# Leaving one half of an inverse transform mirrored, in a kernel of windowed attention beside a long convolution

## The chip, the cores and the metric

The kernel runs on one core of a Trainium2 chip. Its engines have instruction queues of their own and wait for one another by semaphores: TensorE (PE: matrix products, with its weight loads listed as PEld), VectorE (DVE), ScalarE (ACT), GpSimd (POOL) and SyncE (SP). SP, ACT and POOL can start DMA transfers; only those that POOL starts can add to what is in the memory they write. The metric is device time in microseconds (us), as the median of runs.

## The reference

Two independent heads are computed and laid side by side in the output, A in columns 0 to 575, B in columns 576 to 1151. A is attention over a dilated window of 8 keys; B is a convolution along the sequence, by Fourier transforms, times q.

```python
def _A_ref(x, wqkv, wo):
    B, S, D = x.shape
    H = 32; Dh = D // H
    W, dil = 8, 2
    ...
    q, k, v = qkv[0], qkv[1], qkv[2]
    ...
    logits = jnp.einsum("bhsd,bhswd->bhsw", q, kg) * scale
    logits = jnp.where(mask[None, None, :, :], logits, -1e9)
    attn = _softmax(logits, axis=-1)
    o = jnp.einsum("bhsw,bhswd->bhsd", attn, vg)
    return (lambda x, *d: x.transpose(*d))(o, 0, 2, 1, 3).reshape(B, S, D) @ wo

def _B_ref(q, k, v, shift_k, ssm_k, ssm_D):
    ...
    for t in range(ks):
        k_shift = k_shift + k_pad[:, t:t + S, :] * shift_k[:, ks - 1 - t][None, None, :]
    kv = k_shift * v
    L = 2 * S
    ...
    y_f = kv_f * kf_f[None, :, :, :]
    y = (lambda x, s, axes=(-2,-1): jnp.fft.irfft2(x, s=s, axes=axes).astype(jnp.bfloat16))(y_f, (1, L), axes=(1, 2))[:, 0, :S, :]
    y = y + kv * ssm_D[None, None, :]
    return q * y
```

Here kg and vg are the keys and values of the window, gathered by position, and kv_f and kf_f the Fourier transforms of kv and ssm_k, padded to twice the length.

## The kernel before

Everything stays in SBUF. Large tiles are reused by hand: xw, Ks, qk, av, v and TB hold other things in each stage, and a stage that wants a region waits until its last reader is done.

**Head A** runs in the first three quarters: projections (ps_proj), products of q and shifted k on DVE (`logits`) summed over a head by PE (ps_log), softmax, weights of attention spread over partitions by DMA (`spread`), products with v on DVE (`weigh`), summed by PE (ps_acc), and the output product (ps_wo, `outputs`). The two factors of a `weigh` product are v and a spread tile X, and X lies by turns in TB, Ks and qk.

**Head B** cuts the sequence into NBL = 4 blocks of 512 rows. Input blocks (kv, in xw) and filter blocks (in Ks) are folded by their mirror symmetry (`mirror`, `fold_filter`), transformed by PE with a table TX or TK (`x_spectrum`: ps_fx, `filter_spectrum`: ps_fk), and stored as two halves, real and imaginary, a and b. A complex product is done with three real ones, and needs a third array c = a + b of each spectrum, its "third": K0 to K3 are those of Ks, X0 to X3 those of xw. A third is made either on DVE (`add_third`, or in `produce`, line 1244, where it is first needed) or by transfers (`third`, lines 1050 to 1055): SP copies a over c, then POOL adds b to c by an accumulating DMA. The table THIRDS says which, PRE at which step DVE makes those of part 0.

`spectral` then works through output blocks j = 0 to 3, three column groups t of each, and for each the products i = 0 to j: DVE multiplies xw's spectrum i with Ks's spectrum j − i (`products`, line 1099, 2304 elements a partition), into one of a few "homes", regions that have become free, in turn; PE sums them over i into ps_z with identity matrices (`sum_of`, line 1126, 16 matrix products each), ACT copies the sum to Y (line 1139). DVE is up to three products ahead of PE. "Block 2's third product" means i = 2 of j = 2, t = 0.

`inverse` takes Y back to time. With E the transform of the one half of Y and O of the other, the first 256 rows of a block are E + O and the last 256 are E − O in mirrored order. PE first makes E in ps_inv, ACT copies it to A; PE adds O on top, and ACT copies E + O to y[0:2]. Then `back` makes the last rows on PE: with matrices of a flipped identity, flip2 · A − flip · y = flip · (2E − (E + O)) = flip · (E − O), in ps_back, which ACT copies to y[2:4] (line 1206). DVE multiplies by q (the "gate", line 1212) and SP stores the block. For block 3 the columns are done as 384 and 192, the last 192 by `last`, which makes E and O in two PSUM tiles and both halves by ps_back; `gate_last` multiplies straight from PSUM.

The order of work is written by hand: `units` is a queue of PE work (with labels: inv, wo, fx, fk), and `until()` takes from it, at each place where it is called, as many as the next number of the table PLACES. `tasks` holds the gates, done once their time is due by a rough clock; block 2's gate waits in `late` until the last product is made. The steps 1 to 26 of the main loop go through `weigh`, start further spreads and outputs, and from step 21 on run pieces of `spectral` by the table ZMIX. FKS and FXS mix the spectra's units, REGROUP and AT place other pieces. `load_q` loads the blocks of q by POOL, into TB, which is free once the last X in it has been read.

Of the kernel before, what the change touches and what calls it, by code (L numbers as in the profile page):

```python
# [12 lines left out]
ALU = mybir.AluOpType  # L13
# [6 lines left out]
    2, 1, 1, 0, 1, 4,  # L20
# [3 lines left out]
    25, 22,  # L24
)

THIRDS = ((0, 1),), ((0, 2), (1, 2)), ((0, 3), (1, 3))

REGROUP = (
    15, 14,  # L30
# [3 lines left out]
    2, 14, 13, 4, 3, 0, 2, 4, 8, 2, 10, 2, 6, 1, 4, 4, 3, 6, 1, 3, 0, 5, 5, 5, 3, 3, 4, 2, 1, 0, 3, 11, 2, 2, 3,  # L34
    1, 1, 4, 0, 10, 0, 3, 0, 2, 11, 1, 1, 0,
# [3 lines left out]
    5, 1, 0, 0, 0, 0, 0, 0, 0, 0, 0, 0, 0, 0, 0, 3, 0, 0, 0, 0, 0, 0, 0, 0, 0, 0, 0, 0, 0, 0,  # L39
)  # L40
FXS = (
    0, 0, 15, 0, 8, 0, 0, 4, 0,
# [7 lines left out]
    1, 5, 19,  # L50
# [9 lines left out]
def kernel(  # L60
# [186 lines left out]
    def turn_x(h):  # L247
# [15 lines left out]
    flip = main.tile([128, 128], BF16, name="flip")  # L263
    nc.gpsimd.affine_select(flip[:], ones128[:], pattern=[[1, 128]], compare_op=ALU.is_equal, fill=0.0,
                            base=-127, channel_multiplier=1)
# [6 lines left out]
    flipn = main.tile([128, 128], BF16, name="flipn")  # L272
    nc.gpsimd.tensor_scalar(flipn[:], flip[:], -1.0, None, op0=ALU.mult)
# [7 lines left out]
    flip2 = main.tile([128, 128], BF16, name="flip2")  # L281
    nc.gpsimd.tensor_scalar(flip2[:], flip[:], 2.0, None, op0=ALU.mult)
# [371 lines left out]
    def negate(*ms):  # L654
        for m in ms:
            signed.add(m)
            dve(288, lambda: nc.vector.tensor_scalar(minus_of(m), spare(m) if m < 2 else row(m, 0), -0.5 * ROOT, None,
                                                     ALU.mult))
# [384 lines left out]
    def outputs(hh, c):  # L1043
        for sb in (2 * hh, 2 * hh + 1):
            for h in range(2):
                units.append((1.15, partial(output, c, sb, h), "wo"))
# [3 lines left out]
    def third(x, n):  # L1050

        moved.add((bool(x), n))
# [19 lines left out]
    def upper(t, j, a, width, c0, n):  # L1072

        return bass.AP(tensor=t.tensor, offset=t.offset + (BL * j + 320 - 64 * a) * width + c0,
                       ap=[[width, 64], [(64, 192)[a] * width, 2], [1, n]])

    def store_b(j, c0, n, src, h):
        other = nc.scalar if j == NBL - 1 else nc.sync
        if h == 0:
# [266 lines left out]
```

## Time and profile before

| | us |
|---|---|
| three runs | 212.08, 213.55, 212.07 |
| median | 212.08 |
| profiled execution, whole | 212.5 |
| its span | 210.8 |
| ACT busy | 150.5 (71%) |
| POOL busy | 74.0 (35%) |
| DMA, mean rate | 188 GB/s |

The granted clock of PE was 0.998 in the profiled execution. In the profile's rows a line L1099 is line 1099 of the listing above; `out<-in` names tiles; a bracket at the end of a row is the time for which the engine stood idle before it and what ended that, as the profile infers it from semaphores. A row that merges several instructions gives the first one's start and their busy time. The "chain" is the work that ended last, followed back from the end, step by step to what released it. A row of SPq, ACTq or POOL with DMA in it is the issue of a transfer; "to landing" is the time from there until its data are in place.

### The profile page before, as it was taken

What the parts mean: (1) busy time and instruction counts of PE and PEld (TensorE: products, weight loads), DVE (VectorE), ACT (ScalarE), POOL (GpSimd) and SP (SyncE); (2) the same over time, 40 slices, a digit from 0 to 9 for tenths busy, and PEclk for the clock granted to TensorE, in tenths of its full rate; (3) what the DMA queues carried; (4) which work ended last, traced back from release to release, by engine and by line L of the source; (5) the groups of instructions that cost most, each with busy time, mean ns of one, the idle gap of its engine ahead of it and who ended that gap; (6) DMA issues with size and microseconds to landing.
All of it is one profiled execution on the core that took longest, in us unless ns stands there. A gap on an engine that the chain in (4) does not pass through costs nothing.

```text
span 210.8 us, 5106 instructions
## 1 busy us (share of the span) xinstructions
PE 200.1 (95%) x2114; PEld 110.7 (53%) x2122; DVE 193.1 (92%) x146; ACT 150.5 (71%) x218; POOL 74.0 (35%) x111
## 2 busy tenths in 40 slices
PE   7999999999999999899999999999989999999891
PEld 2443443344554656564354666656555666666460
DVE  7989999999999999858889999999999849999981
ACT  3799988657684989986369788855666796775540
POOL 8999993001195516320175000002029004033000
PEclk9999999999999999999999999999999999999999
DMA  6999998999639336999999997587559995985133
GB/s 201 303 328 231 266 342 280 170 192 182 151 75 122 48 40 87 180 181 171 235 225 238 194 234 159 105 208 185 153 223 255 239 322 110 214 243 182 28 113 111
DMA packets 35396, 39.66 MB, mean 188 GB/s; under 512 B 17619, under 2 KB 29007, under 8 KB 35374
## 3 DMA queue, kind: packets, MB, share of 16 engines
q1 hardware_dynamic: 26812, 24.88, 47.2%
q0 software_dynamic: 6096, 11.96, 30.4%
q10 hardware_dynamic: 2466, 2.51, 3.5%
q8 instruction: 16, 0.26, 0.5%
q14 instruction: 6, 0.05, 0.1%
HBM read 13.11 MB, written 4.72 MB: 85 GB/s over the span
## 4 chain that ended last, share of the span: by engine, by line
PE 80%; ACT 10%; DVE 5%; issue 2%; DVEq 0%; ACTq 0%
PE ps_proj L378 16%; PE ps_z L1126 9%; PE ps_wo L1029 8%; PE ps_acc L973 7%; PE ps_inv L1158 7%; PE ps_fx L776 6%; PE ps_log L847 4%; PE ps_proj L500 3%; PE ps_fk L627 3%; PE ps_proj L382 3%; PE ps_proj L389 3%; ACT Ks L695 3%; PE ps_rev L673 2%; PE ps_fk L628 1%; ACT qk L977 1%
## 5 line engine op out<-in xcount | busy, mean ns | idle before, releaser
L378 PE MATMUL ps_proj<-xw 128*128 128x512 bf16 x153 | 37.4, 380 | 0.6 <-issue 0.3
L832 DVE TENSOR_TENSOR av<-qk 128x4096 bf16<-128x4096 bf16 (+1 forms) x16 | 31.7, 2013 | 2.8 <-PE ps_log L847 2.8
L378 PEld LDWEIGHTS <-xw 128*128 128x128 bf16 x160 | 14.0, 97 | 20.5 <-issue 6.2
L1099 DVE TENSOR_TENSOR qk<-xw,Ks 128x2304 bf16<-128x2304 bf16 x14 | 18.5, 1355 | 2.5 <-PE ps_inv L1158 2.4
L1139 ACT ACTIVATE av<-ps_z 128x768 bf16<-128x768 f32 x20 | 15.3, 808 | 6.2 <-PE ps_z L1126 6.2
L414 ACT ACTIVATE qk<-ps_proj 128x1024 bf16<-128x1024 f32 x14 | 14.3, 1023 | 7.6 <-PE ps_proj L389 3.3
L695 ACT ACTIVATE Ks<-ps_fk 128x576 bf16<-128x576 f32 x32 | 18.6, 717 | 1.3 <-PE ps_fk L628 1.3
L577 DVE TENSOR_TENSOR tB<-kj,skb 128x4608 bf16<-128x4608 bf16 (+1 forms) x8 | 19.3, 2417 | 0.1
L778 ACT ACTIVATE xw<-ps_fx 128x576 bf16<-128x576 f32 x32 | 18.4, 666 | 0.0
L776 PE MATMUL ps_fx<-xw,TB 128*128 128x288 bf16 x128 | 18.0, 286 | 0.2
L1055 POOL DMA_DIRECT2D Ks<-Ks x3 | 3.7, 1218 | 41.1 <-PE ps_wo L1029 28.7
L1029 PE MATMUL ps_wo<-qk 128*128 128x288 bf16 x128 | 17.8, 287 | 0.0
L627 PE MATMUL ps_fk<-Ks,TB 128*128 128x384 bf16 x62 | 16.9, 326 | 0.8 <-ACT Ks L695 0.7
L414 ACT ACTIVATE v<-ps_proj 128x1024 bf16<-128x1024 f32 x9 | 9.3, 1029 | 9.3 <-PE ps_proj L378 4.3
L973 PE MATMUL ps_acc<-av,ident 64*64 64x512 bf16 x160 | 15.3, 377 | 0.0
L628 PE MATMUL ps_fk<-Ks,TB 128*128 128x192 bf16 x62 | 15.2, 245 | 0.0
L776 PEld LDWEIGHTS <-TB 128*128 128x128 bf16 x128 | 12.0, 97 | 6.0 <-issue 2.9
L1029 PEld LDWEIGHTS <-qk 128*128 128x128 bf16 x128 | 11.6, 98 | 5.6 <-issue 3.0
L1158 PE MATMUL ps_inv<-av,TI 128*128 128x288 bf16 (+1 forms) x96 | 13.6, 293 | 0.6 <-ACT av L1139 0.6
L1161 ACT ACTIVATE v<-ps_inv 128x576 bf16<-128x576 f32 (+1 forms) x14 | 9.5, 677 | 6.3 <-PE ps_inv L1158 6.3
L977 ACT ACTIVATE qk<-ps_acc 128x1024 bf16<-128x1024 f32 x8 | 8.2, 1024 | 8.0 <-PE ps_acc L973 8.0
L956 DVE TENSOR_TENSOR av<-Ks,v 128x4096 bf16<-128x4096 bf16 x6 | 13.6, 2286 | 0.2 <-PE ps_acc L973 0.2
(199 smaller groups left out, 471.3 us busy)
## 6 DMA issues: line engine op xcount, KB each, us to landing
Ks<-Ks POOLq DMA_DIRECT2D x9, 576.0 KB, 7.1
TB<-av SPq DMA_DIRECT2D x12, 256.0 KB, 5.5
kj<-in_B_k_dram SPq DMA_DIRECT2D x6, 504.0 KB, 6.1
vt<-in_B_v_dram SPq DMA_DIRECT2D x8, 288.0 KB, 5.2
Ks<-av SPq DMA_DIRECT2D x8, 256.0 KB, 5.5
Ks<-Ks SPq DMA_DIRECT2D x3, 576.0 KB, 6.1
Ks<-in_A_x_dram SPq DMA_DIRECT2D x2, 576.0 KB, 5.2
xw<-in_A_wqkv_dram SPq DMA_DIRECT2D x2, 576.0 KB, 5.9
```

Source lines behind the costliest of these rows:

```text
L378: nc.tensor.matmul(ps[:, jp, :], wq(kb, comp, 128 * ct, 128), xT(kb, 1024 * jj + 512 * jp, 512), **se)
L414: nc.scalar.activation(view(t, o + pad + 1024 * jj, [[512, 2], [1, 512]]), ps[:], ACT.Copy)
L577: dve(2304 * n, lambda: nc.vector.tensor_tensor(to, view(kj, row * D, [[D, n], [D, 4], [1, D]]), view(skb, row * D, [[D, n], [0, 4], [1, D ...
L627: nc.tensor.matmul(o[:, 0:2], w, rhs[:, 0:2], start=start, stop=stop)
L695: nc.scalar.activation(view(Ks, k_at(m, cs ^ (m & 1)) + 96 * gi, [[768, 3], [384, 2], [1, 96]]), acc3(ps), ACT.Copy, scale=(PSG, MSG)[cs][ ...
L776: nc.tensor.matmul(ps[:, pm, 0:HD], TX[:, 2 * pm + c, 128 * gi:128 * gi + 128], kv[:, 2 * c + pm, HD * h:HD * h + HD], start=(c == 0), sto ...
L832: return P, at, step, dve(1024 * nj, lambda: nc.vector.tensor_tensor(view(P, at, [[step, 4], [256, nj], [1, 256]]), view(t, o + 256 * hh, ...
L973: nc.tensor.matmul(acc[64 * o:64 * o + 64, h, :], ident[64 * h:64 * h + 64, 64 * h:64 * h + 64], view(P, 256 * u, [[2048, 2], [1, 256]])[6 ...
L1029: nc.tensor.matmul(ps[:, r, 0:HD], oT(hh, 2 * c + r, t)[:, o:o + 128], wo[:, t // 2, t % 2, HD * h:HD * h + HD], start=(t == 0 and h == 0) ...
L1099: r = dve(3 * QTR, lambda: nc.vector.tensor_tensor(pr, view(xw, HB * XG[i] + QTR * t, [[HB, 3], [1, QTR]]), view(Ks, k_at(j - i, 0) + QTR ...
L1126: nc.tensor.matmul(view(acc[r], 512 * h, [[192, 2], [96, 2], [1, 96]])[o:o + 64], w[64 * h:64 * h + 64, 64 * h:64 * h + 64], pr[64 * h:64 ...
L1158: nc.tensor.matmul(ps[:, c, 0:n], TI[:, sl, pm, 128 * c:128 * c + 128], Y(j, pm)[:, sl, c0:c0 + n], start=(pm == 0 and sl == 0), stop=(sl ...
```

## The change

1. **The mirrored half.** `back`, `last`, `quarter` and the flip matrices go. ACT copies E with a scale of 2, so that A = 2E, and DVE makes A − y = E − O, which is left in mirrored order. To match, the rows of q and of the result that belong to the last 256 rows of a block are loaded and stored in mirrored order (`rows` with a negative step), in more and smaller transfers: four for each block of q in place of three, four stores of a block in place of three. In `table_i` the identity's columns are permuted, so that the mirrored halves lie on the same partitions. `last` goes too: both column groups of block 3 run through `unit`, and the last group's gate reads E + O from PSUM.
2. **Thirds.** THIRDS and BY_DMA now name (0, 0), (0, 1), (1, 1) and (1, 2) for transfers at steps 37, 21, 13 and 36; a step above 26 does not occur in the loop, and what is left of the list THIRDS[1] is done after it. PRE is (26, 42).
3. **Signed rows.** `negate` runs on ACT instead of DVE.
4. **Last copies and stores.** The copies of the last sum are divided in halves between ACT and DVE; stores of blocks 2 and 3 are divided between SP, POOL and ACT.
5. **Homes and order.** Products of blocks 2 and 3 get two more homes, (qk, 0) and (qk, HB), and a home is only given out when its last product has been summed (`busy`). Block 3's products are summed together up to the last one (TOGETHER). ZMIX, PRE, REGROUP, PLACES, FKS, FXS and AT have new numbers.

```diff
 ZMIX = (
-    2, 1, 1, 0, 1, 4,
+    3, 1, 0, 0, 1, 5,
 )
 PRE = (
-    25, 22,
+    26, 42,
 )
+TOGETHER = (
+    2, 11,
+)
-THIRDS = ((0, 1),), ((0, 2), (1, 2)), ((0, 3), (1, 3))
+THIRDS = ((0, 0), (0, 1), (1, 1), (1, 2)), ((0, 2), (1, 2)), ((0, 3), (1, 3))
+BY_DMA = (
+    37, 21, 13, 36,
+)
...
@@ table_i
-                                     ident[:], start=True, stop=True, tile_position=(0, 64 * o))
+                                     view(ident, 16, [[32, 4], [-16, 2], [1, 16]]), start=True, stop=True,
+                                     tile_position=(0, 64 * o))
@@ negate
-            dve(288, lambda: nc.vector.tensor_scalar(minus_of(m), spare(m) if m < 2 else row(m, 0), -0.5 * ROOT, None,
-                                                     ALU.mult))
+            nc.scalar.activation(minus_of(m), spare(m) if m < 2 else row(m, 0), ACT.Copy, scale=-0.5 * ROOT)
+            clk["A"] += 0.6
...
+    def rows(t, j, h, e, width, c0, n):
+
+        first, ap = (447 - 128 * e, [[64 * width, 2], [-width, 64]]) if h else (64 - 64 * e, [[width, 64], [128 * width, 2]])
+        return bass.AP(tensor=t.tensor, offset=t.offset + (BL * j + first) * width + c0, ap=ap + [[1, n]])
+
+    def placed(t, h, e):
+        return t[:, 2 + e] if h else t[64 * e:64 * e + 64, 0:2]
 
     def store_b(j, c0, n, src, h):
...
+        for e in range(2):
+            eng = nc.sync if e == 0 or j < NBL - 2 else nc.scalar if c0 else nc.gpsimd
+            eng.dma_start(rows(outf, j, h, e, 2 * D, D + c0, n), placed(src, h, e))
 
     def load_q(j):
...
+        for h in range(2):
+            for e in range(2):
+                nc.gpsimd.dma_start(placed(qB, h, e), rows(qf, j, h, e, D, 0, D))
@@ products
+        if j > 1:
+            homes += ((qk, 0), (qk, HB))
+        if j > 1:
+            need("wo0")
+        while homes[npr[0] % len(homes)] in busy.values():
+            npr[0] += 1
@@ sum_of
-                if (j, t, r) == (NBL - 1, 2, 1):
-                    nc.vector.tensor_copy(y, z)
+                if (j, t) == (NBL - 1, 2):
+                    nc.scalar.activation(y[:, 0], z[:, 0], ACT.Copy)
+                    nc.vector.tensor_copy(y[:, 1], z[:, 1])
@@ inverse
+        def gate():
+            if j < NBL - 1 and c0 == 0:
+                return
+            o, w = (c0, n) if j == NBL - 1 else (0, D)
+            qB, yj, Aj = (t[:, :, o:o + w] for t in (qBs[j], yA[:, j % 2, 0:4, :], yA[:, j % 2, 4:6, :]))
+            lo = box["ps"][:, :, 0:n] if end else yj[:, 0:2]
+            if end:
+                mult(qB[:, 0:2], lo, qB[:, 0:2], 2 * w)
+                store_b(j, o, w, qB, 0)
+            mult(yj[:, 2:4], Aj, lo, 2 * w, ALU.subtract)
...
+            mult(qB, yj, qB, 4 * w)
+            for h in range(2):
+                store_b(j, o, w, qB, h)
...
+            if pm == 0:
+                nc.scalar.activation(A, ps[:, :, 0:n], ACT.Copy, scale=2.0)
                 return
...
+            if not end:
+                nc.scalar.activation(y[:, 0:2], ps[:, :, 0:n], ACT.Copy)
...
-        return [(0.0035 * n, partial(unit, 0), f"inv{j}", ready), (0.0035 * n, partial(unit, 1), f"inv{j}", ready),
-                (0.0018 * n, back, f"inv{j}", ready)]
+        return [(0.0035 * n, partial(unit, pm), f"inv{j}", ready) for pm in range(2)]
@@ spectral
-        if i % 2 and (j, t, i) != todo[-1]:
+        if i % (1, 2, TOGETHER[0], TOGETHER[1])[j] and (j, t, i) != todo[-1]:
```

How the change moves instructions is shown at three places. The first is POOL's queue from the last filter transfers to block 2's thirds; `128x2x1152` is the add of a third, `in_B_q_dram` a load of q. Before:

```order
L714 DMA Ks<-Ks 128x2x1152 x2
L1055 DMA Ks<-Ks 128x2x1152
L1087 DMA TB<-in_B_q_dram 128x2x576
L1089 DMA TB<-in_B_q_dram 64x2x576 x2
L1087 DMA TB<-in_B_q_dram 128x2x576
L1089 DMA TB<-in_B_q_dram 64x2x576 x2
L1055 DMA Ks<-Ks 128x2x1152
L1055 DMA xw<-xw 128x2x1152
```

and after:

```order
L716 DMA Ks<-Ks 128x2x1152 x2
L1058 DMA xw<-xw 128x2x1152
L1058 DMA Ks<-Ks 128x2x1152
L1092 DMA TB<-in_B_q_dram 64x2x576 x2
L1092 DMA TB<-in_B_q_dram 128x1x576 x2
L1092 DMA TB<-in_B_q_dram 64x2x576 x2
L1092 DMA TB<-in_B_q_dram 128x1x576 x2
L1058 DMA Ks<-Ks 128x2x1152
L1058 DMA xw<-xw 128x2x1152
```

X1's add has come in ahead of K1's, and eight loads of q, where six were, stand ahead of K2's and X2's adds.

The second is DVE in blocks 1 and 2: line 1099 (now 1110) are the spectral products, L1244 a third, L1212 the gate, L1164 the gate's operations after the change. Before, from X1 to block 2's gate of block 0:

```order
L1244 TENSOR_TENSOR xw<-xw 128x2304
L1099 TENSOR_TENSOR qk<-xw,Ks 128x2304 x2
L1099 TENSOR_TENSOR Ks<-xw,Ks 128x2304
L1099 TENSOR_TENSOR v<-xw,Ks 128x2304
L1099 TENSOR_TENSOR qk<-xw,Ks 128x2304 x2
L1099 TENSOR_TENSOR av<-xw,Ks 128x2304
L1099 TENSOR_TENSOR v<-xw,Ks 128x2304
L1099 TENSOR_TENSOR qk<-xw,Ks 128x2304
L1212 TENSOR_TENSOR TB<-v,TB 128x2304
```

and after:

```order
L1110 TENSOR_TENSOR qk<-xw,Ks 128x2304 x2
L1110 TENSOR_TENSOR Ks<-xw,Ks 128x2304
L1110 TENSOR_TENSOR v<-xw,Ks 128x2304
L1110 TENSOR_TENSOR av<-xw,Ks 128x2304
L1110 TENSOR_TENSOR qk<-xw,Ks 128x2304 x2
L1110 TENSOR_TENSOR v<-xw,Ks 128x2304
L1164 TENSOR_TENSOR v<-v 128x1152
L1164 TENSOR_TENSOR TB<-v,TB 128x2304
L1110 TENSOR_TENSOR qk<-xw,Ks 128x2304 x2
L1164 TENSOR_TENSOR v<-v 128x1152
L1164 TENSOR_TENSOR TB<-v,TB 128x2304
```

X1 is gone from DVE, each gate has a subtraction of 1152 elements ahead of it, and block 1's gate stands two products behind that of block 0, where before it stood six behind.

The third is ACT at the end: L1139 (now L1152 and, for the last sum, L1149) copies a sum, L1161 (now L1200 for A and L1203 for y) copies ps_inv, L1179 was `last`. Before:

```order
L1206 ACTIVATE v<-ps_back 128x2x288 x2
L1139 ACTIVATE av<-ps_z 128x4x192 x2
L1161 ACTIVATE v<-ps_inv 128x2x384 x2
L1139 ACTIVATE av<-ps_z 128x4x192
L1179 ACTIVATE v<-ps_inv 128x2x192 x2
```

and after:

```order
L1152 ACTIVATE av<-ps_z 128x4x192 x2
L1200 ACTIVATE v<-ps_inv 128x2x384
L1149 ACTIVATE av<-ps_z 128x2x192 x2
L1203 ACTIVATE v<-ps_inv 128x2x384
L1200 ACTIVATE v<-ps_inv 128x2x192
```

The copy of block 3's second 384-wide inverse has moved behind the copies of the last sum, as has that inverse on PE, and the last 192 columns have one copy in place of two.

More of the change, by code (lines that the diff above doesn't have):

```diff
@@ L1277, in spectral @@
                 units.insert(sum(w[2][:3] == "inv" for w in units), u)
+            if new and (j, t) == (NBL - 1, 2):
+                until()
             yield
@@ L1293 @@
             spread(5)
-            for x, m in THIRDS[0]:
+        for at, (x, m) in zip(BY_DMA, THIRDS[0]):
+            if n == at:
                 third(x, m)
         for x in range(2):
-            if n == PRE[x]:
+            if n == PRE[x] and (bool(x), 0) not in moved:
                 add_third(x, 0)
@@ L1305 @@
     for x, n in THIRDS[1]:
-        if x:
-            need(f"fx{n}")
-        third(x, n)
+        if (bool(x), n) not in moved:
+            third(x, n)
     for _ in zs:
```

111 lines of the change are left out of this document (29 added, 82 removed).

## The prediction, on record before the run

> **What bounds the kernel now.** First the page: the busy shares and the chain of work that ended last.
>
> ```profile
> PE 200.1 (95%) x2114; PEld 110.7 (53%) x2122; DVE 193.1 (92%) x146; ACT 150.5 (71%) x218; POOL 74.0 (35%) x111
> PE 80%; ACT 10%; DVE 5%; issue 2%; DVEq 0%; ACTq 0%
> ```
>
> TensorE (PE) carries the chain, but VectorE (DVE) is nearly as full, so work taken from PE is worth only what DVE can follow. Next, the table by stretches, for the part that the change touches (span, then busy time of PE, PEld, DVE, ACT, POOL):
>
> ```profile
> 160.00:180.00 20.00, 20.00 (x280) 13.09 (x279) 16.20 (x14) 15.63 (x24) 5.46 (x6) 1.00 0.92 235
> 180.00:190.00 10.00, 10.00 (x171) 6.83 (x173) 10.00 (x9) 7.20 (x12) 2.00 (x3) 1.00 0.94 237
> 190.00:200.00 10.00, 9.09 (x179) 5.81 (x168) 10.00 (x9) 5.57 (x8) 1.92 (x3) 1.00 0.34 100
> ```
>
> From 160 to 180 DVE has 3.8 us idle; from 180 to 200 none. The order of time shows which idle time that is, and the end:
>
> ```profile
> 166.54 1.35 DVE L1099 TENSOR_TENSOR qk<-xw,Ks 128x2304 bf16<-128x2304 bf16 x1
> 170.28 1.36 DVE L1099 TENSOR_TENSOR qk<-xw,Ks 128x2304 bf16<-128x2304 bf16 x1 [2.40 <-PE ps_inv L1158]
> 171.56 1.35 DVE L1099 TENSOR_TENSOR av<-xw,Ks 128x2304 bf16<-128x2304 bf16 x1
> 174.22 1.36 DVE L1099 TENSOR_TENSOR v<-xw,Ks 128x2304 bf16<-128x2304 bf16 x1 [1.30 <-PE ps_wo L1021]
> ...
> 200.87 1.35 DVE L1212 TENSOR_TENSOR TB<-v,TB 128x2304 bf16<-128x2304 bf16 x1
> 203.13 0.96 DVE L1137 CAST av<-ps_z 128x768 bf16<-128x768 f32 x1 [0.91 <-PE ps_z L1126]
> 204.00 0.55 DVE L1167 TENSOR_TENSOR TB<-v,TB 128x768 bf16<-128x768 bf16 x1
> 204.47 0.95 DVE L1167 TENSOR_TENSOR TB<-ps_back,TB 128x768 bf16<-128x768 f32 x1
> 206.19 1.02 DVE L1167 TENSOR_TENSOR TB<-ps_back,TB 128x384 bf16<-128x384 f32 x2 [0.78 <-PE ps_back L1185]
> ```
>
> The products at 170.28, 171.56 and 174.22 are block 2's first three. The first is the first to read part 2's third spectrum in Ks (K2 below), the third the first to read it in xw (X2). The view puts their waits down to PE, but the transfers' view says otherwise. GpSimd's queue, then the times to landing: of the Ks add alone, of both, of the next pair.
>
> ```profile
> 156.74 0.74 POOL L1087 DMA_DIRECT2D TB<-in_B_q_dram  x1 [11.97 <-DVE qk L956]
> ...
> 159.39 1.24 POOL L1089 DMA_DIRECT2D TB<-in_B_q_dram  x2
> 160.58 1.30 POOL L1055 DMA_DIRECT2D Ks<-Ks  x1
> 161.34 1.78 POOL L1055 DMA_DIRECT2D xw<-xw  x1
> DMA to landing us min/median/max: 9.5/9.5/9.5
> DMA to landing us min/median/max: 9.5/11.1/12.7
> DMA to landing us min/median/max: 5.4/6.5/7.7
> ```
>
> K2: 160.58 + 9.5 = 170.1, and the product starts at 170.28. X2: 161.34 + 12.7 = 174.0, and the product starts at 174.22. Both waits end as a third spectrum lands; I take them as waits for transfers. After 174.22 DVE runs without a gap to the end of the last product at 200.9.
>
> **The change, part by part.** *The mirrored half on PE.* All ps_back work goes. From the chain:
>
> ```profile
> 170.88 0.37 PE ps_back L1199 x8
> 172.55 0.25 PE ps_back L1199 x8
> 189.24 2.75 PE ps_z L1126 x64
> 200.25 1.41 PE ps_inv L1158 x8
> ```
>
> Six groups for blocks 0 to 2, two by 0.37 + 0.25, make 1.9 us, and block 3's first about 0.3: 2.2 us less on PE ahead of the end. ScalarE loses six copies, but is at 71% and bounds nothing here. So PE alone would allow −2.2, and a little more by the end, below. (The row of ps_z gives 2.75 / 4 = 0.7 for the sum of one product.)
>
> *DVE.* Costs of what comes and goes, each row with its mean ns; the row with 0.69 is a 128x1024 operation on SBUF data:
>
> ```profile
> L1244 DVE TENSOR_TENSOR xw<-xw 128x2304 bf16<-128x2304 bf16 x1 | 1.4, 1352 | 0.0
> L1244 DVE TENSOR_TENSOR Ks<-Ks 128x768 bf16<-128x768 bf16 x2 | 1.1, 554 | 0.0
> L657 DVE TENSOR_SCALAR Ks<-Ks x3: 290/293/325, 54.6 to 63.3; 1x576 bf16<-1x576 bf16 x3
> 79.58 0.69 DVE L876 TENSOR_TENSOR av<-av 128x1024 bf16<-128x1024 bf16 x1
> ```
>
> Ahead of block 2 two whole sums go (part 1 in xw, now by transfer; part 0 in xw, now in three pieces) and two 768 pieces come: −1.35 − 1.35 + 2 × 0.55 = −1.6. Behind it, the gates of blocks 0 and 1 get a subtraction of 1152 elements each, 0.7 by the 1024 row: +1.4. Both now stand on a DVE that has no gap. The four signed rows, 4 × 0.3 = −1.2, lie before 88 us, and the waits between them and the spectral part are these:
>
> ```profile
> 90.31 1.23 DVE L832 TENSOR_TENSOR av<-qk 128x2048 bf16<-128x2048 bf16 x1 [1.38 <-PE ps_log L847]
> 93.27 1.23 DVE L892 TENSOR_TENSOR av<-av 128x2048 bf16<-128x2048 bf16 x1 [1.74 <-ACT av L889]
> 106.68 2.29 DVE L956 TENSOR_TENSOR av<-TB,v 128x4096 bf16<-128x4096 bf16 x1 [0.62 <-PE ps_log L847]
> ```
>
> DVE waits there for PE and ScalarE, so 1.2 us saved ahead become 1.2 us more of waiting: nothing. On ScalarE the first pair of rows waits for the filter's load, and it does so in the queue, right behind this copy; POOL's row shows when the load has landed:
>
> ```profile
> 47.97 1.02 ACT L414 ACTIVATE qk<-ps_proj 128x1024 bf16<-128x1024 f32 x1 [1.02 <-PE ps_proj L378]
> 50.60 0.54 POOL L736 DMA_DIRECT2D Ks<-Ks  x1 [7.98 <-DMA Ks<-in_B_ssm_k_dram]
> ```
>
> So ScalarE stands from 49.0 to 50.6, 1.6 us in which the copies behind it, which free PSUM for PE, are late. Its queue had waits of about 1 us there (the 1.02 in the row), so I take 0, at most +1.0. One more 2048 product goes to v instead of av, so that one of the waits of about 0.6 for ps_log can fall away: 0 to −0.6. But the added transfer of X1 now stands on SyncE's queue ahead of the last spread of attention weights, which landed just in time before: last issue at 134.99, 6.7 us, 141.7, against a product at 141.79.
>
> ```profile
> 134.99 1.34 SPq L934 DMA_DIRECT2D TB<-av  x1
> DMA to landing us min/median/max: 6.7/6.7/6.7
> 141.79 2.29 DVE L956 TENSOR_TENSOR qk<-TB,v 128x4096 bf16<-128x4096 bf16 x1
> ```
>
> The earlier product would find it missing: 0 to +1. For the early part I take half of the gain, −0.3.
>
> *K2 and X2.* DVE now finishes with the spread weights 1.35 − 0.55 = 0.8 earlier, so GpSimd's loads of q start at 155.9 instead of 156.74. They are eight instead of six; by the mean of 0.62 (half of 1.24), 5.0 us, to 160.9. K2's add then goes out at 160.9 and X2's at 161.65, hardly other than now: the loads of q eat the lead. What gets better is the traffic. The copies below are issued when block 0's second product has been summed; the order puts that sum one weighing earlier, near 150 instead of 153.92. And the order moves 36 of the last 60 ps_wo products behind block 1, with their stores. The bounds for landing are the undisturbed pair (5.4, 7.7) and the present one (9.5, 12.7). I take the middle, 7.5 and 10.2: half of what crowds them is still there (the q loads).
>
> ```profile
> 153.92 0.52 SPq L1054 DMA_DIRECT2D Ks<-Ks  x1
> ```
>
> K2 lands at 168.4, X2 at 171.9. DVE wants block 2 at 167.9 − 1.6 = 166.3 and waits 2 us; the third product starts at 172.0, not 174.2: −2.2. With +1.4 for the subtractions the last product ends at 200.9 − 0.8 = 200.1. If K2 and X2 land as late as now, X2 comes at 161.65 + 12.7 = 174.35, which gives +0.2 + 1.4 = +1.6; if like the next pair, 169.35, −4.9 + 1.4 = −3.5, more than PE allows.
>
> The Trainium skill (SBUF — State Buffer, section "Who interferes with whom") warns that a DMA issued by GpSimd is starved of its descriptors while VectorE runs in a two-port mode. [...]
>
> *The end.* Before, the last sum ends just ahead of the CAST of 203.13, and DVE's last work at 206.19 + 1.02 = 207.2: 4.15 us, and 6.3 from the end of the last product at 200.9. Now PE runs block 3's second 384-wide inverse (1.41) behind the last sum, ScalarE copies it (0.81, the row below), DVE does a subtraction and two products of 768 (3 × 0.5), then from PSUM product, subtraction (2 × 0.5) and one product (0.3): with 0.4 for the hand-overs between engines, 5.0 us, +0.85. But those 1.41 us no longer stand ahead of the sum, which makes PE's allowance 2.2 + 1.4 − 0.85 = 2.75; and the last sum, 0.7 us, can follow the product at once: 0.7 + 5.0 = 5.7 after the last product, where 6.3 stood. I take −0.4, for the sums of the two products before it are in PE's queue too. The halved copies (0.5 for 0.96) are hidden behind the 1.41. Behind the last operation stand the stores, one on SP and one on ScalarE, as now:
>
> ```profile
> L1161 ACT ACTIVATE v<-ps_inv 128x768 bf16<-128x768 f32 x2 | 1.6, 811 | 2.9 <-PE ps_inv L1158 2.9
> 207.25 0.59 SPq L1083 DMA_DIRECT2D out_dram<-TB  x1
> ```
>
> GpSimd's two stores of the 384 part go out 1.3 us earlier (the three operations on the 192 part), and its cost of 0.62 a transfer leaves them inside that: nothing. The Trainium skill (DMA: Bandwidth & Descriptors, section "Specifications") gives GpSimd's path 1 us to the first byte against 0.6, which would use 0.4 of the lead; no run here shows it yet.
>
> Sum: −0.3 − 2.2 + 1.4 − 0.4 = −1.5. The profiled execution took 212.5 (span 210.8), so 211.0; the median of the runs is 212.08, 0.4 lower, and on that scale the forecast is 210.6.
>
> **The rivals.** *PE held the buffers, as the waits' view says.* The change gives two more homes for products from block 2 on and moves PE work back, so both waits (3.7) would go: −3.7 + 1.4 = −2.3, which PE allows, and with −0.3 and −0.4 −3.0: 209.1. For it: the label; against: two landings that fit within 0.2 us. An early landing gives the same time.
>
> *K2 and X2 land as late as now, and the subtractions come on top:* +1.6 in place of −0.8, so −0.3 + 1.6 − 0.4 = +0.9, or 213.0; without the early and the last gain, which are both unsure, 213.7. For it: eight q loads stand ahead in the same queue, and each microsecond of late landing is paid in full from 166.3 on. It decides, that is brings more time than before, when X2 lands after 173.5.
>
> *Block 1's gate becomes a wait.* It moves ahead of block 2's last third, and needs PE's run of 32 ps_inv, four times 1.41 × 288 / 384 = 1.06 us, behind the second product. That product ends at 171.1; 0.7 + 4.2 + 1.0 for the copy gives 177.0, and DVE is there at 178.3. PE must be 1.3 us late before it costs anything; 1 us more gives 211.6.
>
> *The change does not do what it says:* only part 1 in xw is new by transfer; the entries 37 and 36 of the new table are never reached by a loop that ends at 26, and part 0 in Ks is still summed twice. That is in the sum.
>
> **How the numbers follow.** Forecast, 0.45: 210.6, own range 209.6 to 211.7. PE held the buffers, or early landing, 0.27: 209.1. Late landing, 0.15: 213.0 to 213.7. The gate's wait, or a late spread at 141, 0.13: 211.6. The range of 208.5 to 213.3 leaves out the lower tail of the first rival and half of the late landing, under 2 in 10. About 1% (2.1 us) is what a measurement tells from no change. Faster than 209.96 are the first rival and a fifth of the forecast, 0.36; slower than 214.2 is only the far end of late landing, 0.08; within, 0.56.
>
> **What would show it.** No ps_back rows; two subtractions near 0.7 us; X2's landing near 172 and block 2's third product at once behind it, DVE without a gap from there; the last sum within 1 us of the last product. Wrong if block 2 waits while its thirds have landed, if DVE waits ahead of 144 for the spread weights, or if the end takes over 6.5 us from the last product.

## The result, and the profile after

The changed kernel takes 229.39 us (median of 3 runs, 228.87 to 231.50) where the kernel before, on the same chip, takes 212.07 (4 runs): a ratio of 1.082 with a 95% interval of 1.072 to 1.092. A run more than 1.5% above the fastest of its kernel counts as slow and is left out of the medians and ranges from here on; with its one such run, 232.41, the changed kernel's median is 230.44. It is 17.3 us slower; the forecast was 210.6 with a range to 213.3. The profiled execution took 231.5 us, its span is 229.8.

In its listing the lines have moved: products of `products` are L1110 (1099 before), GpSimd's sums of third spectra L1058, loads of q L1092, stores of head B L1086, the weighing L958, the operations of the gates L1164. First the page's busy shares and its chain by engine:

```profile
PE 200.3 (87%) x2040; PEld 111.3 (48%) x2050; DVE 193.8 (84%) x149; ACT 149.3 (65%) x216; POOL 76.6 (33%) x117
PE 43%; DMA 21%; DVE 13%; ACT 7%; issue 5%; POOL 2%; SPq 2%; DVEq 0%; POOLq 0%; ACTq 0%
```

PE and DVE are as busy in microseconds as before (200.1 and 193.1), in a span 19 us longer. PE's share of the chain fell from 80% to 43%, and transfers, which had no share that the page listed, hold 21%. So the time went into waiting for DMA. DVE's order of time in the changed kernel shows where (start, duration, in brackets the idle time before the row and what ended it):

```profile
143.47 2.29 DVE L958 TENSOR_TENSOR qk<-TB,v 128x4096 bf16<-128x4096 bf16 x1 [2.90 <-DMA TB<-av]
...
175.84 1.36 DVE L1110 TENSOR_TENSOR av<-xw,Ks 128x2304 bf16<-128x2304 bf16 x1 [7.10 <-DMA Ks<-Ks]
177.11 1.35 DVE L1110 TENSOR_TENSOR qk<-xw,Ks 128x2304 bf16<-128x2304 bf16 x1
181.46 1.36 DVE L1110 TENSOR_TENSOR qk<-xw,Ks 128x2304 bf16<-128x2304 bf16 x1 [2.99 <-DMA xw<-xw]
...
184.00 0.75 DVE L1164 TENSOR_TENSOR v<-v 128x1152 bf16<-128x1152 bf16 x1
...
215.99 0.36 DVE L1164 TENSOR_TENSOR TB<-v,TB 128x384 bf16<-128x384 bf16 x1
```

Three waits: 2.9 us for the last spread weights, 7.1 for K2, 3.0 for X2. Block 2's third product starts at 181.46 instead of 174.22. The last product ends at 209.8 instead of 200.9 (8.9 us later), and DVE's last operation at 216.35, 6.6 behind it, where 6.3 stood before.

GpSimd's queue in the changed kernel, with the sums of K2 and X2:

```profile
163.34 1.30 POOL L1058 DMA_DIRECT2D Ks<-Ks  x1
164.13 1.76 POOL L1058 DMA_DIRECT2D xw<-xw  x1
```

And the transfers' view of two of its lines, the time from issue to landing of the eight q loads issued from 157 to 163, then of the four sums of third spectra issued from 163 to 182:

```profile
DMA to landing us min/median/max: 3.3/8.7/9.4
DMA to landing us min/median/max: 6.3/9.4/17.3
```

X2's sum is issued at 164.13 and lands 17.3 us later, at 181.4: the product at 181.46 begins at once. K2's lands after 12.3. The forecast had 10.2 for X2's landing and 12.7 as its late bound.

The rest of the loss stands behind all computing. The stretches of the changed kernel's end (span, then busy time of PE, PEld, DVE, ACT, POOL, the granted clock, the share of the 16 DMA engines that was busy, GB/s):

```profile
219.00:222.00 3.00, 0.00 (x0) 0.00 (x0) 0.00 (x0) 0.00 (x0) 0.00 (x0) 0.50 0.36 100
222.00:225.00 3.00, 0.00 (x0) 0.00 (x0) 0.00 (x0) 0.00 (x0) 0.00 (x0) 0.50 0.14 38
225.00:229.80 4.80, 0.00 (x0) 0.00 (x0) 0.00 (x0) 0.00 (x0) 0.00 (x0) 0.50 0.09 21
```

And the view of the stores' line over the last twelve stores, six of them of the mirrored half: SP's issues (shortest, middle and longest in ns, first and last start), and the times to landing of all twelve:

```profile
L1086 SPq DMA_DIRECT2D out_dram<-TB x6: 515/786/2413, 211.9 to 218.7; - x6
...
DMA to landing us min/median/max: 3.1/8.7/9.6
```

From DVE's end at 216.35 to the span's end are 13.4 us, where the kernel before had 210.8 − 207.2 = 3.6: 9.8 us more. The DMA share is what names the cause: 0.14 of 16 engines is 2.2 engines. The last store is issued at 218.7, so from 222 on nothing waits for an issue, and no more than 38 GB/s flow: two or so engines carry what is left. The share holds that level: taken microsecond by microsecond it stays at 0.14 to 0.15 from 222 to 227, and from 228 on the DMA engines are idle. (The clock of 0.50 there, and 0.967 in the mean, goes with a PE that has nothing to do; it is no cause.)

What has two of something is the new access pattern. `rows` gives a transfer of the mirrored half as [[64·w, 2], [−w, 64], [1, n]] on the memory side: 2 runs of 64 rows, each run backwards. The Trainium skill (DMA: Bandwidth & Descriptors, section "Why a DMA increments its semaphore by 16 and not by 1") says that a transfer is split over the largest number of engines, up to 16, that divides the slowest dimension of both sides; here that would be 2. The experiments test this theory (FEW ENGINES) against others: that walking rows backwards is slow, that GpSimd's queue is, and that the order of the transfers is to blame.

### The profile page after: what moved, and what is told of

Same layout as the page of the kernel before. It is cut to its first block, busy times and chain, and to the rows that moved or that the text cites. A ratio compares the mean times of both kernels' runs of the same rounds, so it can differ in the third digit from the quotient of the medians.

```text
span 229.8 us, 4968 instructions
## 1 busy us (share of the span) xinstructions
PE 200.3 (87%) x2040; PEld 111.3 (48%) x2050; DVE 193.8 (84%) x149; ACT 149.3 (65%) x216; POOL 76.6 (33%) x117
## 3 DMA queue, kind: packets, MB, share of 16 engines
q1 hardware_dynamic: 26362, 25.03, 43.3%
q0 software_dynamic: 8784, 13.07, 31.0%
## 4 chain that ended last, share of the span: by engine, by line
PE 43%; DMA 21%; DVE 13%; ACT 7%; issue 5%; POOL 2%; SPq 2%; DVEq 0%; POOLq 0%; ACTq 0%
PE ps_proj L379 15%; DMA xw<-xw 8%; DMA out_dram<-TB 7%; DMA TB<-av 4%; PE ps_fx L778 3%; PE ps_proj L502 3%; DVE av L958 3%; DMA TB<-in_B_q_dram 3%; PE ps_acc L975 3%; PE ps_proj L383 2%; PE ps_proj L390 2%; PE ps_log L849 2%; POOL TB L1092 2%; PE ps_fk L629 2%; DVE av L834 2%
## 5 line engine op out<-in xcount | busy, mean ns | idle before, releaser
L834 DVE TENSOR_TENSOR av<-qk 128x4096 bf16<-128x4096 bf16 (+1 forms) x15 | 30.4, 2073 | 1.0 <-PE ps_log L849 1.0
L1110 DVE TENSOR_TENSOR qk<-xw,Ks 128x2304 bf16<-128x2304 bf16 x16 | 21.1, 1354 | 3.0 <-DMA xw<-xw 3.0
L1152 ACT ACTIVATE av<-ps_z 128x768 bf16<-128x768 f32 x19 | 14.5, 808 | 12.0 <-PE ps_z L1138 12.0
L1092 POOL DMA_DIRECT2D TB<-in_B_q_dram x16 | 11.5, 725 | 31.9 <-DMA out_dram<-TB 16.9
L629 PE MATMUL ps_fk<-Ks,TB 128*128 128x384 bf16 x62 | 16.4, 326 | 0.7 <-ACT xw L780 0.4
L1195 PE MATMUL ps_inv<-av,TI 128*128 128x288 bf16 (+2 forms) x112 | 15.2, 290 | 1.2 <-ACT v L1200 0.6
L1195 PEld LDWEIGHTS <-TI 128*128 128x128 bf16 x128 | 11.9, 99 | 6.9 <-issue 3.8
L958 DVE TENSOR_TENSOR av<-Ks,v 128x4096 bf16<-128x4096 bf16 x6 | 13.6, 2285 | 0.0
```

The lines of the kernel that those rows point to most:

```text
L629: nc.tensor.matmul(o[:, 0:2], w, rhs[:, 0:2], start=start, stop=stop)
L834: return P, at, step, dve(1024 * nj, lambda: nc.vector.tensor_tensor(view(P, at, [[step, 4], [256, nj], [1, 256]]), view(t, o + 256 * hh, ...
L958: r = dve(4096, lambda: nc.vector.tensor_tensor(view(P, 0, [[2048, 2], [256, W], [1, 256]]), X, view(v, voff + 2 + 256 * hh, [[512, 2], [2 ...
L1110: r = dve(3 * QTR, lambda: nc.vector.tensor_tensor(pr, view(xw, HB * XG[i] + QTR * t, [[HB, 3], [1, QTR]]), view(Ks, k_at(j - i, 0) + QTR ...
L1195: nc.tensor.matmul(ps[:, c, 0:n], TI[:, sl, pm, 128 * c:128 * c + 128], Y(j, pm)[:, sl, c0:c0 + n], start=(pm == 0 and sl == 0), stop=(sl ...
```

## Experiments

The comparisons are with the kernel before on the same chip, whose medians lay between 212.07 and 212.26.

### e1: all mirrored transfers in ascending rows

```diff
-        first, ap = (447 - 128 * e, [[64 * width, 2], [-width, 64]]) if h else (64 - 64 * e, [[width, 64], [128 * width, 2]])
+        first, ap = (256 + 128 * e, [[width, 128]]) if h else (64 - 64 * e, [[width, 64], [128 * width, 2]])
```

> The changed kernel with one thing different: the mirrored half of q, and of the result, is moved in ascending row order, so that the memory side of those transfers is one run of 128 rows and not 2 runs of 64 that each run backwards. Partitions, bytes, number of transfers, queues and every computing instruction stay; which rows land on which partition is wrong. FEW ENGINES (a transfer whose slowest dimension counts 2 is carried by 2 DMA engines, not 16): X2 lands near 172-174 and (2,0,2) no longer waits, the last product ends near 203 (the 2.9 us wait for the spread weights may stay), DVE's last end to the span's end falls from 13.4 to about 4 us: 210 to 215 us. GPSIMD QUEUE (what POOL issues is slow, or POOL is late): 229 to 232. ORDER (X1's copy ahead of the spread, eight q loads ahead of the sums of K2 and X2): up to the last product as in the changed kernel (209.7), the stores' tail gone if that is another cause: 220 to 223.

216.06 us (215.37 to 216.50), ratio 1.018 (1.016 to 1.020). 13.3 of the 17.3 us are gone, by an edit that moves the same bytes with the same instructions. DVE's order of time in e1:

```profile
143.07 2.29 DVE L958 TENSOR_TENSOR qk<-TB,v 128x4096 bf16<-128x4096 bf16 x1 [2.13 <-DMA TB<-av]
...
173.95 1.36 DVE L1110 TENSOR_TENSOR qk<-xw,Ks 128x2304 bf16<-128x2304 bf16 x1 [1.20 <-DMA xw<-xw]
```

The landings in e1 of the same q loads and third spectra as above:

```profile
DMA to landing us min/median/max: 3.6/4.8/5.1
DMA to landing us min/median/max: 5.4/7.7/9.8
```

And two stretches of e1's end:

```profile
209.00:210.00 1.00, 0.00 (x0) 0.00 (x0) 0.00 (x0) 0.00 (x0) 0.00 (x0) 1.00 0.90 249
211.00:214.00 3.00, 0.00 (x0) 0.00 (x0) 0.00 (x0) 0.00 (x0) 0.00 (x0) 0.50 0.00 0
```

The q loads land in 4.8 us instead of 8.7. The sums of K2 and X2 are issued within 0.5 us of where the changed kernel issues them, but land after 7.1 and 9.8 us instead of 12.3 and 17.3, X2 at 173.9, and the last stores, mirrored and not, run on 0.90 · 16 = 14 engines at 249 GB/s. GPSIMD QUEUE and ORDER fall as main causes. The time missed FEW ENGINES' range by 1.1 us, and the last row shows a piece of it: from 211 the DMA engines are idle, and the span still goes on for 3.2 us (e11).

### e2 and e3: only the loads, only the stores

The same edit, taken only where `width` is D (the loads) or only where it is 2 · D (the stores).

> As e1, but only the loads of q in ascending order; the stores of the mirrored half stay backwards in 2 runs of 64. FEW ENGINES: K2 and X2 land about as in e1, last product near 203, and the stores' tail stays at 12 to 14 us behind DVE's last end: 219 to 225 us. GPSIMD QUEUE and ORDER: 229 to 232, with X2 at 181.

> As e1, but only the stores in ascending order; the loads of q stay backwards in 2 runs of 64. FEW ENGINES: X2 still lands near 181 and the last product ends near 208 to 210, the stores' tail falls to about 4 us: 219 to 223 us. GPSIMD QUEUE: 229 to 232 (two stores of 384 and two of 576 are still POOL's).

Loads alone: 225.29 us (223.62 to 226.25), ratio 1.061 (1.056 to 1.065), 0.3 us over FEW ENGINES' range, with the last product's end at 202.8 and a tail of 13.6. Stores alone: 220.64 (219.33 to 221.43), ratio 1.039 (1.035 to 1.043), as FEW ENGINES has it. The loads' pattern costs 229.4 − 225.3 = 4.1 us and the stores' 229.4 − 220.6 = 8.7, each to a microsecond or so, as the runs of one kernel spread by 2 to 3 us; their sum, 12.8, is about what e1 took away in one (13.3). Two things were missed in e3: the last product ended at 207.1, not at 208 to 210, and X2 landed at 178.8, not near 181. The stores' pattern is not the reason for the latter, for no store of head B is issued before X2 lands (the first at 183.5 here, at 186.2 in the changed kernel). Four profiled kernels have the loads on two engines, and X2 landed between 178.4 and 181.4 in them; what makes this difference is not shown.

### e4 and e12: two and four runs, ascending

e4 takes (256 + 64 e, [[128 · w, 2], [w, 64]]), e12 (256 + 32 e, [[64 · w, 4], [w, 32]]), for loads and stores: as in e1 no row runs backwards, but the slowest dimension counts 2, then 4.

> As e1 in that all rows ascend, but each of the transfers takes two runs of 64 rows that lie 128 rows apart, so that the slowest dimension counts 2 as in the changed kernel and only the direction within a run is other. FEW ENGINES: as the changed kernel, 228 to 233 us, X2 near 181, a tail of 12 to 14 us. BACKWARD ROWS (it is the direction in which the rows are walked that makes the transfers slow): as e1, 210 to 215.

> As the kernel of two ascending runs, but each transfer of the mirrored half takes four runs of 32 rows, 64 rows apart: its slowest dimension counts 4 (rows placed wrong). FEW ENGINES, as many as that count: four engines carry each transfer. If the excess over e1 (14.4 us with 2 engines) goes with 1/engines, it is (1/4 - 1/16) / (1/2 - 1/16) = 0.43 of 14.4 = 6.2 us: 220 to 224, tail behind DVE's last end 7 to 9 us. ONLY ROWS IN ONE RUN ARE FAST (any break in the rows costs the same): 229 to 232.

e4: 230.26 us (229.17 to 231.58), ratio 1.085 (1.081 to 1.090), the changed kernel's time. Going backwards costs nothing that can be measured. Inside e4's trace two details differ from what was expected: X2 lands at 179.2, and DVE's last end comes at 217.7, after a wait of 3.7 us for which the view names no releaser, so that the tail behind it is 9.9 us and not 12 to 14. From the last product's end to the span's end it is the same as in the changed kernel, 20.1 us against 20.0.

e12: 222.52 (220.70 to 222.75), ratio 1.045 (1.042 to 1.049), with a tail of 8.8 us. The estimate by 1/engines before the run was 216.1 + 6.2 = 222.3; with 13.3 in place of 14.4 for the excess it is 221.8. With runs that spread by 2 us this does not fix the law, but it rules out that any break in the rows costs the same. A stretch of e12 behind all computing:

```profile
214.00:216.00 2.00, 0.00 (x0) 0.00 (x0) 0.00 (x0) 0.00 (x0) 0.00 (x0) 0.50 0.26 70
```

0.26 of 16 is 4.2 engines, at 70 GB/s where two gave 38. (From 212 to 214, while GpSimd's stores are in flight as well, the share is 0.58.) The landings of the last twelve stores, in e12:

```profile
DMA to landing us min/median/max: 3.2/5.5/6.8
```

and in e1:

```profile
DMA to landing us min/median/max: 2.3/2.7/3.2
```

The median landing is 8.7, 5.5 and 2.7 us as the slowest dimension counts 2, 4 and 128. The rule cited above from the Trainium skill (DMA: Bandwidth & Descriptors, same section) agrees with these traces at all three (2.2, 4.2 and 14 engines). One thing goes along with the number of engines: GpSimd's queue moves 8784, 7552 and 6624 packets in the three kernels, the additional ones nearly all under 512 bytes. SP's and ACT's stores have no such packets more (SP's queue moves 26362 with 2 against 26460 with 128), so for them these are not the cause; for the q loads the two were not separated.

### e8: the mirrored stores all on GpSimd

```diff
-            eng = nc.sync if e == 0 or j < NBL - 2 else nc.scalar if c0 else nc.gpsimd
+            eng = nc.gpsimd if h else nc.sync if e == 0 or j < NBL - 2 else nc.scalar if c0 else nc.gpsimd
```

> The changed kernel, whole and right, with every store of the mirrored half issued by POOL instead of by SP, ACT and POOL. FEW ENGINES, AND ALWAYS THE SAME TWO for what SP and ACT issue (the Trainium skill, DMA: Bandwidth & Descriptors, section on why a DMA increments its semaphore by 16, says the lowest-numbered there and consecutive ones from a moving cursor for GpSimd's queue): the last stores of two engines each run beside one another instead of behind one another, and the tail behind DVE's last end falls from 13.4 to 7 to 9 us: 222 to 226 us. FEW ENGINES, BUT SPREAD EITHER WAY: the tail stays at 12 us or more: 229 to 232. POOL'S QUEUE IS SLOW: over 232.

226.80 us (226.14 to 226.84), ratio 1.067 (1.065 to 1.069). Faster by 2.6 us than the changed kernel, but the tail is 224.4 − 213.1 = 11.3 us, neither 7 to 9 nor over 12. In the profiles DVE's last end is 3.3 us earlier, but 3.1 of that is X2's landing at 178.4, ahead of all stores of head B, which this edit did not touch. What the tail consists of, two stretches of e8's end show:

```profile
219.00:221.00 2.00, 0.00 (x0) 0.00 (x0) 0.00 (x0) 0.00 (x0) 0.00 (x0) 0.50 0.46 103
221.00:224.40 3.40, 0.00 (x0) 0.00 (x0) 0.00 (x0) 0.00 (x0) 0.00 (x0) 0.50 0.02 4
```

GpSimd's last four stores are all of the mirrored half, and with little else in flight they keep 0.46 · 16 = 7.4 engines busy, at 103 GB/s, where those of SP and ACT in the changed kernel kept 2.2. So GpSimd's transfers of two engines each run beside one another, and SP's and ACT's share the same two or so. The transfers end before 222, within 9 us of DVE's last end, as the first theory has it; the rest of the tail is a drain of GpSimd's queue of 9.8 us, from 213.8 to 223.6 (on such drains see e11). The view counts busy engines and does not name them, so which two SP and ACT take is not shown.

### e5: X1 on DVE again

e1 with the entry (1, 1) of THIRDS and its 13 of BY_DMA taken out.

> e1 (mirrored half moved in ascending rows, which rows land on which partition is wrong) with X1 no longer made by transfers: its copy ahead of the last spread and its sum on POOL are gone, and DVE adds it whole (1.36 us) between block 1's products. COLLISION (X1's two transfers of 576 KB share the DMA engines with the spread's weights, which therefore land at 143.0 instead of about 141): DVE's wait of 2.1 us ahead of the last weighing falls to under 0.8, what follows it starts 1.3 to 2 us earlier, and the 1.36 us of the sum is paid again or hidden ahead of X2's landing: 214.0 to 216.0 us. SPREAD LATE ANYWAY (SP's own order or the weights' maker sets it): the wait stays near 2 us and the time is 216.5 to 217.5.

214.71 us (214.30 to 215.43), ratio 1.011 (1.009 to 1.012), e1 less 1.35. The row that waited 2.13 us in e1, in e5's trace:

```profile
141.85 2.29 DVE L958 TENSOR_TENSOR qk<-TB,v 128x4096 bf16<-128x4096 bf16 x1 [0.56 <-DMA TB<-av]
```

COLLISION holds: the last spread is issued no earlier than in e1 (134.8 against 134.1) but lands in 6.9 us instead of 8.8. X1's transfers held it up, and what that cost was more than the sum of 1.36 us that they took from DVE. More came of it than the time shows: X2's sum now lands after 8.3 us, DVE does not wait for it, and block 2's third product starts at 171.0 instead of 173.95. But then DVE stands for block 1's gate, which gives back 2.0 of these 3.0 us:

```profile
178.92 0.76 DVE L1164 TENSOR_TENSOR v<-v 128x1152 bf16<-128x1152 bf16 x1 [2.00 <-ACT v L1203]
```

### e6 and e7: the q loads behind the sums of K2 and X2

In e1 and in the kernel before, the two calls `load_q(0)` and `load_q(1)` go behind the loop over THIRDS[1].

> e1 with POOL's eight q loads issued behind the sums of K2 and X2 instead of ahead of them (same transfers, other order on one queue; rows placed as in e1). THE LOADS' ISSUE HOLDS THE SUMS: K2's sum is issued near 158 instead of 162.8, X2 lands 3 to 5 us earlier than 173.9, the 1.2 us wait of (2,0,2) goes and the time falls by 0.8 to 1.5 us: 214.5 to 215.3. COPIES OR BUFFERS SET IT: X2's sum starts little earlier, or (2,0,2) waits for something else at the same moment: 215.7 to 216.5.

> The kernel before, whole and right, with only POOL's six q loads issued behind the sums of K2 and X2. In its trace (2,0,2) starts at 174.2 after a gap of 1.4 to 2.4 us. X2'S LANDING SETS THE GAP: it shrinks by 1 us or more and the time falls to 210.5 to 211.3. PE SETS IT (the product's buffer comes free only when PE has read it): the product starts at 174.2 again and the time is 212.0 to 212.5. If the q loads now land behind DVE's first gate at about 176, slower: 213 or more.

e6 is slower, 217.51 us (216.93 to 218.42), ratio 1.025 (1.022 to 1.027); neither theory had that. X2's wait did go, but the transfers now came upon the stores of head A. ScalarE's copy of the output product stood for one of them, with the copies that PE needs behind it in the queue:

```profile
168.44 0.65 ACT L1038 ACTIVATE TB<-ps_wo 128x576 bf16<-128x576 f32 x1 [4.59 <-DMA out_dram<-TB]
```

e7 is the telling one: 212.50 us (212.07 to 214.97), ratio 1.003 (1.000 to 1.005). DVE's rows in it:

```profile
167.01 2.62 DVE L1099 TENSOR_TENSOR qk<-xw,Ks 128x2304 bf16<-128x2304 bf16 x2
169.55 1.35 DVE L1099 TENSOR_TENSOR av<-xw,Ks 128x2304 bf16<-128x2304 bf16 x1
171.95 1.36 DVE L1099 TENSOR_TENSOR v<-xw,Ks 128x2304 bf16<-128x2304 bf16 x1 [1.05 <-PE ps_z L1126]
...
181.41 2.63 DVE L1099 TENSOR_TENSOR qk<-xw,Ks 128x2304 bf16<-128x2304 bf16 x2 [1.76 <-PE ps_z L1126]
...
197.91 2.62 DVE L1099 TENSOR_TENSOR qk<-xw,Ks 128x2304 bf16<-128x2304 bf16 x2
```

Block 2 starts at 168.3 (the second of the pair at 167.01) instead of 170.28, its third product at 171.95 instead of 174.22. So the waits in the kernel before were waits for transfers; the time of 210.5 to 211.3 that went with that theory did not follow. 9 us later DVE stands 1.76 us for PE, and the last product ends at 200.5 instead of 200.9: of 2.3 us, 0.4 are left. PE was next. Here the label is right, as PE's own rows show: 24 matrix products of an inverse (ps_inv) hold PE from 177.21 for 3.12 us, and only then does it sum the product that lies in qk, from 180.53 to about 181.3. DVE's next product, which goes into qk, starts at 181.41.

### e9: the signed rows on ScalarE, alone

The kernel before, with the change's two lines in `negate`.

> The kernel before, whole and right, with only the signed rows moved from VectorE to ScalarE. In the changed kernel the first product with the signed filter begins at 105.4 us instead of 106.7. THE ROWS ALONE GIVE THAT: DVE arrives up to 1.3 us earlier there, but the spread's weights land near 141 to 142 all the same, so the end gains at most 0.5 us: 211.5 to 212.2. NOT THEIRS (order tables or the other edits give it, or ACT becomes late at the copies behind): 212.1 to 212.8.

213.87 us (212.39 to 215.23), ratio 1.007 (1.004 to 1.010): slower, a miss for both. In e9's trace, ScalarE's second row of the pair, and the copy behind it:

```profile
49.61 0.68 ACT L657 ACTIVATE Ks<-Ks 1x576 bf16<-1x576 bf16 x1 [2.10 <-DMA Ks<-in_B_ssm_k_dram]
50.20 1.00 ACT L414 ACTIVATE qk<-ps_proj 128x1024 bf16<-128x1024 f32 x1
```

The stall that the prediction bounded by 1.0 us is there, with 2.1. It reaches DVE at 65.25 as a wait of 2.5 us for a copy of ScalarE's, and DVE's first product with spread weights (line 956; the expectation calls it that with the signed filter) starts at 108.32 instead of 106.68. In the changed kernel the same rows run at 49.03 without a wait, and that product at 105.40: they come later in ScalarE's queue there (49.03 and not 46.85) and find the load landed.

### e10, e11 and e13: what is left

e10 is e5 with PRE set to (42, 42), so that the loop never makes K0's second sum. e11 is e5 with block 2's and 3's last stores on SP and ACT:

```diff
-            eng = nc.sync if e == 0 or j < NBL - 2 else nc.scalar if c0 else nc.gpsimd
+            eng = nc.sync if e == 0 or j < NBL - 1 else nc.scalar
```

e13 is both together.

> e5 (mirrored half in ascending rows, placed wrong; X1 on DVE) without the second, whole sum of K0 on DVE (1.36 us) that the changed kernel makes behind the three quarter sums of the same K0. DVE BOUNDS BLOCK 1: all behind it starts about 1.3 us earlier and the time falls by 0.8 to 1.4 us: 213.3 to 213.9. SOMETHING ELSE BOUNDS IT (PE's reading of the products, X2's landing): 214.3 to 215.

> e5 with the four last stores that POOL issues (two of 576, two of 384) moved to SP and ACT. In e5 the span ends 4.6 us behind SP's last issue, in the kernel before 3.0 us behind its last. GPSIMD'S QUEUE MAKES THE END LONGER: the gap falls to about 3 us, 213.0 to 213.9. NUMBER OF LAST STORES MAKES IT LONGER (eight for block 3's two pieces where there were six): no change or slower by what ACT's two more issues cost, 214.5 to 215.5.

> e11 and e10 together: the changed kernel with its mirrored transfers in ascending rows (placed wrong), X1 on DVE, K0 summed once and the last stores on SP and ACT, so that of the change mainly the missing flip products, the subtractions in the gates and the signed rows on ScalarE are left. COSTS ADD UP (each of the three was paid apart): 212.9 - 0.8 = 212.1, within 211.5 to 212.6, no faster than the kernel before, since DVE pays for the subtractions what it wins ahead of them. THE FLIPS' END IS WORTH SOMETHING of itself: 210.0 to 211.4.

e10: 213.90 us (213.06 to 214.98), ratio 1.007 (1.005 to 1.010), 0.8 less than e5, at the edge of DVE BOUNDS; its interval and e5's overlap a little, so the 0.8 is rough. e11: 212.91 (212.14 to 213.26), ratio 1.002 (1.000 to 1.003), 1.8 less than e5 and 0.1 under the range of GPSIMD'S QUEUE. What makes GpSimd's stores dear at the end is a row of its queue in the launch line, in e1's trace (shortest, middle and longest in ns, first and last start):

```profile
L1328 POOLq DRAIN  x3: 46/108/5749, 207.7 to 213.9; - x3
```

and in e11's:

```profile
L1328 POOLq DRAIN  x3: 46/102/5753, 190.3 to 210.8; - x3
```

A drain of 5.75 us stands behind GpSimd's last transfer. In e11 it begins at 190.3 (in the kernel before at 192.7) and is over before the end; in e1 it begins at 207.7 and outlasts the landings.

e13: 211.87 us (211.10 to 213.69), ratio 0.997 (0.995 to 0.999). COSTS ADD UP: without its four dear parts the change is worth 0.3%, with rows that are placed wrong; so no kernel here that keeps its rows right beats the kernel before.

## Why the prediction was wrong

| part | how measured | us |
|---|---|---|
| q loads on 2 engines | changed kernel − e2 | 4.1 |
| mirrored stores on 2 engines | changed kernel − e3 | 8.7 |
| both together | changed kernel − e1 | 13.3 |
| X1 by transfers | e1 − e5 | 1.35 |
| GpSimd's last stores | e5 − e11 | 1.8 |
| K0's second sum | e5 − e10 | 0.8 |
| what is left | e13 − before | −0.2 |

13.3 + 1.35 + 1.8 + 0.8 − 0.2 = 17.05, of 17.3. The rows are steps of one chain of kernels, so this sum tests only whether the parts of e10 and e11 add up: together (e13) they are 2.8, one by one 2.6.

- **The step that failed: a transfer of a new shape was priced by a transfer of the old shape.** "They are eight instead of six; by the mean of 0.62 (half of 1.24), 5.0 us" counts what the q loads cost GpSimd to issue, and the landings of K2 and X2 were bounded by pairs that had run beside loads of the old shape. The issue came out at 0.73 each; the landing, which had no term, is 8.7 us instead of 4.8 (e1), and the sums of K2 and X2 behind them in the queue landed after 12.3 and 17.3 us instead of 7.1 and 9.8. That these waited for the very engines on which the loads sat is the likely reason, but no view names a transfer's engines. The slowest dimension stood in the diff.
- **The stores behind the last operation, "as now",** failed in the same way, and cost more: 8.7 us. Nothing computes behind them, so all of it is paid. The sentence beside it, that GpSimd's two stores of 384 lie inside their lead and cost nothing, failed by the drain, which shows once the rows ascend (e5 against e11).
- **K2 and X2, −2.2.** The reading of the waits as transfers was right, against the profile's label (e7). The gain was wrong even in e1, where the rows ascend: X2 landed at 173.9, by 9.8 us where 10.2 was taken, because its sum was issued at 164.1 and not at 161.65. With X1 back on DVE (e5) it landed by 170.4, the q loads still ahead of it, and with the loads behind it (e6) the wait went, too. And in the kernel before (e7), PE took 1.9 of 2.3 us back.
- **Late spread at 141.** Named and bounded, 0 to +1; the trace shows a wait of 2.9, e1 one of 2.1, and e5 prices it at 1.35 us net. The mechanism was right, the size too small. It set back the issue of the q loads, too: 157.6 in the changed kernel and not 155.9.
- **Subtractions, +1.4.** Right: 0.75 each. In e1, from the start of block 2's third product to the end of the last one, 28.3 us stand where 26.7 stood, +1.6.
- **The end, −0.4.** It came out at +0.1 in e1 (6.4 us from the last product to DVE's last end, before 6.3), and at 6.6 us in the changed kernel, past the 6.5 that were named as a sign of being wrong. The last sum does follow within 1.0 us, but 5.4 us come behind it, not 5.0. This is a slip in the adding: the terms named (1.41, 0.81, 3 × 0.5, 2 × 0.5 and 0.3) make 5.0 by themselves, and the 0.4 for the hand-overs was left out; with it they are the 5.4 that the trace shows.
- **The early part, −0.3.** DVE came 1.3 us earlier at 105.4, by the rows and the tables together (e9), and lost that at the spread.
- **The rivals.** Late landing had the right place and its own point, X2 after 173.5, was passed by 7.9 us; but its end, 12.7 us, was a row of the old shape, and the price of 213.7 with it. PE as the holder of the buffers falls with e7, as the cause of those two waits. Block 1's gate did become a wait, of 2.0 us, where X2 came early (e5), and cost nothing in the changed kernel, where DVE was late. That K0 is summed twice stood in the prediction, and e10 prices it.

## What to carry to other kernels

Read each changed transfer's pattern before its bytes: count the slowest dimension on both sides, and where it is as small as the 2 and 4 here, price the transfer by its share of the DMA engines, on its own landing, on what lands beside it, and in full where it is the last thing that runs. A landing taken from a row holds only for transfers of that shape. And when a wait ahead of a busy engine goes, look for the engine that is next before the gain is booked; here PE took it back within 10 us.

## What the runs showed of the hardware

- Behind all computing the DMA share, times 16, came out near the count of the slowest dimension of SP's and ACT's stores: 2.2 where it counts 2 (222 to 227 in the changed kernel), 4.2 with 4 (214 to 216 in e12), 14 with 128 (209 to 210 in e1). The excess time with 4 was 6.5 us, where 1/engines gives 5.7.
- GpSimd's transfers of two ran beside one another on 7.4 engines (e8, 219 to 221), SP's and ACT's together on 2.2.
- Rows that a transfer walks backwards cost no more than rows walked forwards (e4, 230.26 us against 229.39, both with runs that spread by over 2 us).
- A drain stands behind GpSimd's last transfer: 5.75 us in e1 and e11, 5.78 in the kernel before, but 9.3 in the changed kernel and 9.8 in e8, where GpSimd's last transfers had two engines. It cost nothing where it began at 190.3 (e11), and 1.8 us where GpSimd issued some of the last stores (e5).
- Open: a mirrored order of rows whose slowest dimension counts more than 2 was not tried, nor is it shown which engines a transfer of two takes.
